# Moving rows of a zero store from behind a GpSimd copy to in front of it

## The chip, the cores and the metric

The kernel runs on one core of a Trainium2 chip. The metric is the device time of one execution in microseconds (us): the median of several runs, beside the profile of one more execution. Engines are named as in the profile: PE (TensorE), DVE (VectorE), ACT (ScalarE), POOL (GpSimd), SP (SyncE, which here does nothing but issue transfers). Data move in DMA transfers; a transfer is split into packets, which run on the core's 16 DMA engines. A transfer signals its end on a semaphore.

## The reference: what is computed

A decoding step of an attention block over a sliding window of cached keys and values, beside a gated feed-forward block, and the gradients of the sum of both with respect to eight inputs. Cut to what matters:

```python
x = A_x                                   # (4, 1, 512)
xn = _layernorm(x, axis=-1)
out = x + _A_ref(xn, A_k_cache, A_v_cache, A_wq, A_wo) \
        + _B_ref(xn, B_w_gate, B_w_up, B_w_down)
# _A_ref: only the last W = 1024 of 4096 cached keys take part
k = jnp.repeat(k_cache[:, :, Sk - W:, :], rep, axis=1)
v = jnp.repeat(v_cache[:, :, Sk - W:, :], rep, axis=1)
...
_out, _vjp = jax.vjp(_f, ...)             # outputs: out and the gradients
```

Two of the nine outputs are the gradients of the two caches, `out_2` (keys) and `out_3` (values), each of 4 batches x 8 heads x 4096 keys x 128 numbers of 2 bytes. The first 3072 keys of each head lie outside the window, so their gradient is zero and must be written as zeros: 50 MB of the 81 MB that the kernel writes.

## The kernel before, in words

First comes the feed-forward block (forward and gradients), then the attention in four passes of the loop over `t`, each with two heads of the cache: `kv_steps` (scores), `softmax`, `kv_steps` again, `softmax_d`, `odq`, and `dvdk` and `dw`, whose pieces are put on a list (`bg`) and called between other work by `tick`. All loads and stores go out in the order of the program text, since the schedule is written by hand (`manual_schedule`). SP issues nearly all of them, from its own queue (q1 in the profile); GpSimd issues the later weight loads and the stores of this change on another (q0).

The zeros come from one tile in on-chip memory, `ztile`, 128 partitions x 6144 numbers of zeros. `zlist` holds 32 entries, each two heads of `out_2` or `out_3`: 1536 KB. `zero(n)` takes the next n and has SP store them; calls of it are strewn over the whole kernel. Thirty of the 32 go out so. `zero_15` (L166 to L187), called once in the last pass (L763), takes the last two entries out of the list, four heads of `out_3` of the last batch, called h = 0 to 3 here. It works with units of 192 keys (`KR`): the first `k0` = 2880 keys are 15 such rows, one unit is left of each head.

- Of h = 0, 1 and 2 the first 2880 keys are copied by GpSimd from the heads of `out_2[0]` that were zeroed long before: 15 rows x 3 heads x 49,152 bytes, from memory to memory (the 15-row copy).
- The unit of 192 keys left of each of these heads is stored from `ztile`, partly by GpSimd, in rows of 16 keys (4096 bytes), partly by SP at the end of the program, 16 rows of some keys each.
- h = 3 is stored whole by SP at the end, in 128 rows of 24 keys.

`rest(eng, n, h, k0, w)` is one such store: `n` rows of `w` keys of head `h`, from key `k0`. With fewer than 128 rows it reads every eighth partition of `ztile`. In the kernel before, GpSimd issues a store of 5 rows (80 keys of h = 0), the copy, and a store of 12 rows (the 192 keys of h = 1). `zero_15` returns a list of functions, called behind the last pass (L781, after `tick(len(bg))` and `zero(len(zlist))`), in which SP stores h = 3, the other 112 keys of h = 0, and the 192 keys of h = 2. `store` (L100 to L107) is the helper through which each goes, so in the profile all of them stand at L103. The stores of the results proper (`stg_dv`, `stg_dk`, `osb_o`, `osb_q`) come from the pieces, also at L103.

Of the kernel before, what the change touches and what calls it, by code (L numbers as in the profile page):

```python
# [14 lines left out]
P = 128  # L15
# [3 lines left out]
def kernel(  # L19
# [28 lines left out]
    nc = tc.nc  # L48

    B, Sq, D = A_x.shape  # L50
    _, G, Sk, Dh = A_k_cache.shape
# [4 lines left out]
    K0 = Sk - W  # L56
# [43 lines left out]
    def store(eng, out, in_, kind):  # L100

        eng.nop()
        d = eng.dma_start(out=out, in_=in_)  # L103
        for k in ("rest", "zeros") if kind == "rest" else ("rest",):
            tc.declare_no_dep(d.ins, group=k, reason="stores write disjoint parts of the outputs")
        tc.add_to_no_dep_group(kind, d.ins)
        return d  # L107
# [50 lines left out]
    ztile = const.tile([P, ZW], BF16, name="ztile")  # L158
# [7 lines left out]
    def zero_15():  # L166


        last = [z for z in zlist if z[0] is out_3][-2:]
        for z in last:  # L170
            zlist.remove(z)
        b, g = last[0][1:]
        assert last[1][1:] == (b, g + ZR)
        dst = out_3[b, g:g + 2 * ZR]
        KR = K0 // 16
        k0 = 15 * KR

        def rest(eng, n, h, k0, w):
            store(eng, dst[h, k0:k0 + n * w, :].rearrange("(m j) d -> m (j d)", m=n), ztile[0:n if n == P else 8 * n - 7:1 if n == P else 8, 0:w * Dh],
                  "zeros")  # L180

        rest(nc.gpsimd, 5, 0, k0, 16)
        s_, d_ = (x[0:3, 0:k0, :].rearrange("g (m j) d -> m g (j d)", m=15) for x in (out_2[0], dst))
        store(nc.gpsimd, d_, s_, "zeros")
        rest(nc.gpsimd, 12, 1, k0, 16)
        return [lambda: rest(nc.sync, P, 3, 0, K0 // P), lambda: rest(nc.sync, 16, 0, k0 + 80, 7),
                lambda: rest(nc.sync, 16, 2, k0, 12)]  # L187


    nc.gpsimd.memset(ztile[:], 0.0)  # L190
# [512 lines left out]
    for f4 in range(NF4):  # L703
        held = {}
        n = min(4, NF - 4 * f4)
# [34 lines left out]
    with tc.tile_pool(name="kv_b", bufs=GP, reuse_waits="tile") as kv_b, \  # L740
# [7 lines left out]
        for t in range(NT):  # L748
# [13 lines left out]
            if t == NT - 1:  # L762
                rest = zero_15()  # L763
# [81 lines left out]
```

## Time and profile before

| what | value |
|---|---|
| median of three runs | 284.18 us (284.09 to 284.64) |
| the profiled execution | 284.17 us |
| its span (first to last instruction) | 282.4 us |
| PE, DVE, ACT, POOL busy | 72%, 58%, 42%, 15% of the span |
| DMA | 112.12 MB, mean 397 GB/s; busy share 0.9 or more in 36 of 40 slices |
| SP's queue (q1) and GpSimd's (q0) | 101.28 and 8.57 MB |
| GpSimd's issues: 5 rows, copy, 12 rows | at 224.43, 224.98 and 225.61 us |
| last compute instruction (`dx_b`, DVE) | ends at 260.8 us |
| SP's last four issues | 266.09, 266.69, 268.01 and 269.26 us |
| end of SP's waiting for the last landings | 281.2 us |

How to read it: the span runs from the first to the last instruction of one execution, times are counted from its start. A line such as "out_dram<-ztile POOLq DMA_DIRECT2D x1, 48.0 KB, 16.9" is one kind of transfer: what it writes and reads, the engine whose queue issued it, how many, the size, and the us from its issue to its landing. `out_dram<-out_dram` is the copy. The packet records of the trace list each packet's queue, start, duration and bytes, but not which of the 16 DMA engines moved it; this can be followed from the order of sizes, since an engine takes up its next packet when the one before ends.

### The profile page before, as it was taken

The numbers are of one execution on the slowest core, as the hardware profiler recorded it, in microseconds if no ns is written. First come the engines' busy times: TensorE is split into PE (matmuls) and PEld (weight loads), VectorE is DVE, ScalarE is ACT, GpSimd is POOL, SyncE is SP. The second block draws the span as 40 slices with busy tenths as digits, with TensorE's granted clock in tenths as the row PEclk, the third lists the DMA queues.
The fourth block names the chain that finished last, engine by engine and source line by source line (L and its number), as shares of the span: only waits on it lengthen the run. The fifth ranks groups of instructions, "written<-read, shape, count | busy, mean of one in ns | idle before, by whom it ended". The sixth has DMA issues, their size and how long they took to land.

```text
span 282.4 us, 6862 instructions
## 1 busy us (share of the span) xinstructions
PE 202.5 (72%) x2962; PEld 138.7 (49%) x2972; DVE 164.4 (58%) x313; ACT 117.7 (42%) x219; POOL 41.9 (15%) x43
## 2 busy tenths in 40 slices
PE   0274799949789889998999199898999599272000
PEld 0263576735456675556765066676555574031000
DVE  7947546645776655577666158767677638178000
ACT  2031486635035418753547155353866048161000
POOL 8600000007002250002340000232000600000000
PEclk9999589986999999999999869999999979958555
DMA  7999999999999999999999999999899998999990
GB/s 265 395 375 430 430 426 419 425 424 414 379 393 429 412 425 421 422 421 421 415 422 414 418 425 423 422 370 399 367 371 414 393 396 357 424 430 427 410 417 38
DMA packets 19613, 112.12 MB, mean 397 GB/s; under 512 B 1746, under 2 KB 4594, under 8 KB 11347
## 3 DMA queue, kind: packets, MB, share of 16 engines
q1 hardware_dynamic: 17664, 101.28, 87.2%
q0 software_dynamic: 1760, 8.57, 7.7%
q10 hardware_dynamic: 160, 1.84, 1.8%
q8 instruction: 23, 0.38, 0.5%
q14 instruction: 6, 0.05, 0.0%
HBM read 32.89 MB, written 81.01 MB: 403 GB/s over the span
## 4 chain that ended last, share of the span: by engine, by line
PE 43%; DMA 26%; DVE 16%; ACT 4%; issue 2%; SPq 0%; DVEq 0%; ACTq 0%
DMA out_dram<-stg_dv 13%; PE T_ps L302 8%; PE kv_ps L507 6%; DMA wd_sb<-in_B_w_down_dram 6%; PE S_ps L368 5%; PE od_ps L473 5%; DMA out_dram<-osb_g 4%; DMA out_dram<-osb_d 3%; DVE T_sb L98 3%; PE dwq_ps L543 2%; DVE dS_s L390 2%; PE acc_ps L279 2%; DVE P_s L390 2%; PE dwo_ps L528 2%; PE pT_ps L302 2%
## 5 line engine op out<-in xcount | busy, mean ns | idle before, releaser
L98 DVE COPY T_sb<-T_ps 128x1024 bf16<-128x1024 bf16 x64 | 44.1, 689 | 26.9 <-PE T_ps L302 26.7
L97 ACT CAST stg_dk<-kv_ps 128x512 bf16<-128x512 f32 x52 | 29.0, 589 | 33.5 <-DMA out_dram<-stg_dv 14.3
L97 ACT CAST stg_dv<-kv_ps 128x512 bf16<-128x512 f32 x51 | 28.1, 588 | 25.1 <-PE kv_ps L507 24.6
L507 PE MATMUL kv_ps<-qmr,dS_s 128*128 128x512 bf16 x62 | 23.3, 412 | 13.3 <-ACT stg_dk L97 12.6
L486 POOL TENSOR_TENSOR o_s<-od_r,msk_r 128x512 bf16<-128x512 bf16 x8 | 9.1, 1158 | 110.4 <-DVE od_r L478 81.1
L302 PE MATMUL T_ps<-ident,vb 128*128 128x128 bf16 x256 | 20.5, 226 | 0.6 <-DVE T_sb L98 0.4
L302 PE MATMUL T_ps<-ident,kb 128*128 128x128 bf16 x256 | 20.6, 226 | 0.2 <-issue 0.2
L302 PEld LDWEIGHTS <-kb 128*128 128x128 bf16 x256 | 17.6, 102 | 4.5 <-issue 1.5
L302 PEld LDWEIGHTS <-vb 128*128 128x128 bf16 x256 | 17.4, 102 | 5.0 <-issue 3.2
L507 PE MATMUL kv_ps<-domr,P_s 128*128 128x512 bf16 x58 | 19.7, 382 | 0.1
L97 ACT CAST osb_q<-dwq_ps 128x512 bf16<-128x512 f32 x25 | 14.6, 586 | 8.6 <-PE dwq_ps L543 7.6
L352 POOL TENSOR_TENSOR domr<-r,msk 128x1024 bf16<-128x1024 bf16 x4 | 7.6, 1892 | 71.2 <-DVE r L349 65.1
L97 ACT CAST osb_g<-dwg_ps 128x512 bf16<-128x512 f32 (+1 forms) x25 | 12.3, 545 | 12.5 <-PE dwg_ps L696 5.7
L98 DVE CAST stg_dk<-kv_ps 128x512 bf16<-128x512 f32 x12 | 8.1, 689 | 14.0 <-DMA out_dram<-stg_dv 13.4
L97 ACT CAST osb_o<-dwo_ps 128x512 bf16<-128x512 f32 x24 | 13.9, 586 | 4.6 <-PE dwo_ps L528 3.8
L98 DVE COPY wgT<-wgT_ps 128x1024 bf16<-128x1024 bf16 x14 | 9.6, 687 | 7.3 <-PE wgT_ps L302 7.3
L507 PEld LDWEIGHTS <-dS_s 128*128 128x128 bf16 x64 | 6.2, 101 | 14.5 <-issue 13.4
L368 PE MATMUL S_ps<-T_sb,qm 128*32 128x256 bf16 x128 | 12.7, 387 | 0.6 <-DVE T_sb L98 0.5
L368 PE MATMUL S_ps<-T_sb,dom 128*32 128x256 bf16 x128 | 12.7, 387 | 0.1
L528 PE MATMUL dwo_ps<-dyr,o_s 128*128 128x512 bf16 x32 | 12.6, 420 | 0.3 <-ACT stg_dk L97 0.2
L98 DVE COPY woT<-woT_ps 128x1024 bf16<-128x1024 bf16 x16 | 11.0, 687 | 2.9 <-PE woT_ps L302 2.5
L543 PE MATMUL dwq_ps<-od_r,xnm 128*128 128x256 bf16 x64 | 11.9, 285 | 0.2 <-ACT osb_q L97 0.2
(190 smaller groups left out, 384.6 us busy)
## 6 DMA issues: line engine op xcount, KB each, us to landing
out_dram<-ztile SPq DMA_DIRECT2D x30, 1536.0 KB, 19.4
kb<-in_A_k_cache_dram SPq DMA_DIRECT2D x8, 1024.0 KB, 20.2
vb<-in_A_v_cache_dram SPq DMA_DIRECT2D x8, 1024.0 KB, 21.7
out_dram<-stg_dv SPq DMA_DIRECT2D x8, 1024.0 KB, 16.6
out_dram<-stg_dk SPq DMA_DIRECT2D x8, 1024.0 KB, 19.4
out_dram<-osb_o SPq DMA_DIRECT2D x8, 512.0 KB, 16.1
out_dram<-osb_q SPq DMA_DIRECT2D x8, 512.0 KB, 19.3
out_dram<-osb_g SPq DMA_DIRECT2D x8, 448.0 KB, 11.8
```

The costliest lines, as they stand in the source:

```text
L97: return nc.scalar.copy(out=out, in_=in_)
L98: return nc.vector.tensor_copy(out=out, in_=in_)
L279: nc.tensor.matmul(ps[:, c, :], lhsT=lf(c), rhs=rhs, start=(k == 0), stop=(k == len(terms) - 1))
L302: nc.tensor.transpose(ps[:, i, :], a, ident[:])
L352: nc.gpsimd.tensor_tensor(out=mr[:].rearrange("p g q d -> p (g q) d"), in0=r4[:, k, :].unsqueeze(1).broadcast_to([P, SL, Dh]), in1=msk[:]. ...
L368: nc.tensor.matmul(ps[b * RB:(b + 1) * RB, :], lhsT=zt[:, b * GP + g, c0:c0 + RB], rhs=T_sb[:].rearrange("p (x b) -> p b x", b=B)[:, b, :] ...
L390: nc.vector.scalar_tensor_tensor(out=out[:], in0=src[:].unsqueeze(2).broadcast_to([P, WQ, B]), scalar=rr[:, 0:1], in1=mskb[:].unsqueeze(1) ...
L473: nc.tensor.matmul(od_ps[g * 32:g * 32 + B * rep, k, g, :], lhsT=cols[:, jj, g * NQ + q, :], rhs=blks[(t, g)][:, j, :], start=(j == 0), st ...
L486: nc.gpsimd.tensor_tensor(out=o_s[:, g], in0=rows[:, g].unsqueeze(1).broadcast_to([P, rep, Dh]), in1=msk_r[:].unsqueeze(2).broadcast_to([P ...
L507: nc.tensor.matmul(mps[:].rearrange("p q d -> p (q d)"), lhsT=src[:, j * P:(j + 1) * P], rhs=mr[:, g].rearrange("p q d -> p (q d)"), start ...
L528: nc.tensor.matmul(mps[:], lhsT=o_s[:, g].rearrange("p r d -> p (r d)")[:, i:rep * Dh:rep], rhs=dyr[:], start=True, stop=True)
L543: nc.tensor.matmul(mps[:, i].rearrange("p g d -> p (g d)"), lhsT=xnm[:, i2 * 2 + i, c * P:(c + 1) * P], rhs=dq_r[:].rearrange("p g d -> p ...
```

## The change

GpSimd issues stores of 9 rows (144 keys of h = 0) and 8 rows (128 keys of h = 1) and then the copy; nothing behind it. What is left of the three units goes out on SP at the end: 16 rows of 3 keys (48 keys of h = 0), of 4 keys (64 keys of h = 1) and of 12 keys (192 keys of h = 2), behind the 128 rows of h = 3. GpSimd's rows of 4096 bytes are 17 in both kernels, and SP's bytes are the same; SP has one transfer more. SP's stores of 16 rows read partitions 0 to 15 of `ztile` instead of every eighth; GpSimd's still read every eighth. The other engines' instructions and their order are the same.

```diff
         k0 = 15 * KR
+        used = [0, 0, 0]
 
         def rest(eng, n, h, k0, w):
-            store(eng, dst[h, k0:k0 + n * w, :].rearrange("(m j) d -> m (j d)", m=n), ztile[0:n if n == P else 8 * n - 7:1 if n == P else 8, 0:w * Dh],
-                  "zeros")
-
-        rest(nc.gpsimd, 5, 0, k0, 16)
+            src = ztile[0:8 * n - 7:8] if n < 16 else ztile[0:n]
+            store(eng, dst[h, k0:k0 + n * w, :].rearrange("(m j) d -> m (j d)", m=n), src[:, 0:w * Dh], "zeros")
+
+        for h, n in enumerate((9, 8)):
+            rest(nc.gpsimd, n, h, k0, 16)
+            used[h] = n * 16
         s_, d_ = (x[0:3, 0:k0, :].rearrange("g (m j) d -> m g (j d)", m=15) for x in (out_2[0], dst))
         store(nc.gpsimd, d_, s_, "zeros")
-        rest(nc.gpsimd, 12, 1, k0, 16)
-        return [lambda: rest(nc.sync, P, 3, 0, K0 // P), lambda: rest(nc.sync, 16, 0, k0 + 80, 7),
-                lambda: rest(nc.sync, 16, 2, k0, 12)]
+        return [lambda: rest(nc.sync, P, 3, 0, K0 // P)] + [
+            lambda h=h: rest(nc.sync, 16, h, k0 + used[h], (KR - used[h]) // 16) for h in range(3)]
```

## The prediction, made before the result was known

> **What bounds the kernel now.** I read the page from its end backwards, since the change touches only the last zero stores. First the stretches of the last 20 us (columns: stretch, its length, busy us and count of each engine, the granted clock PEclk, the mean busy share of the 16 DMA engines, GB/s):
>
> ```profile
> 262.00:273.00 11.00, 0.00 (x0) 0.00 (x0) 0.00 (x0) 0.00 (x0) 0.00 (x0) 0.50 1.02 420
> 273.00:276.00 3.00, 0.00 (x0) 0.00 (x0) 0.00 (x0) 0.00 (x0) 0.00 (x0) 0.50 0.84 347
> 276.00:277.20 1.20, 0.00 (x0) 0.00 (x0) 0.00 (x0) 0.00 (x0) 0.00 (x0) 0.50 0.14 58
> 277.20:280.40 3.20, 0.00 (x0) 0.00 (x0) 0.00 (x0) 0.00 (x0) 0.00 (x0) 0.50 0.06 25
> 280.40:282.40 2.00, 0.00 (x0) 0.00 (x0) 0.00 (x0) 0.00 (x0) 0.00 (x0) 0.50 0.00 0
> ```
>
> From 262 us no compute engine has work; the DMA engines drain stores. From 277.2 the share is 0.06, which is one engine in sixteen: **for 3.2 us a single DMA engine is still writing, and the kernel ends when it does.** The transfers of that stretch say what it writes:
>
> ```profile
> DMA packets 15, 0.08 MB, mean 25 GB/s; under 512 B 3, under 2 KB 4, under 8 KB 13
> ...
> q1 hardware_dynamic: 15, 0.08, 5.9%
> ```
>
> q1 is SP's queue: the share this engine has of SP's last four stores. Every one of those is cut evenly over the sixteen engines, so this engine has no more to do, it is late. I followed the packet records (start, duration, bytes) backwards, each engine's SP packets being the same row of sizes in the same order. Fifteen engines end at 273.35 to 277.19 us, fourteen of them between 275.3 and 277.2; the last ends at 280.44. From 242 us on it has no gap at all, and it was late before: of the 512 KB store issued at 219.54, the median engine lands at 222.21 and the last at 227.35, 5.1 behind. So the end moves by what is added to or taken from **this one engine's packets**, called the late engine below. Anything else has slack.
>
> Now the transfers of GpSimd's queue, 224.3 to 225.7 (operation, count, KB, us from issue to landing):
>
> ```profile
> out_dram<-out_dram POOLq DMA_DIRECT2D x1, 2160.0 KB, 16.7
> out_dram<-ztile POOLq DMA_DIRECT2D x1, 48.0 KB, 16.9
> out_dram<-ztile POOLq DMA_DIRECT2D x1, 20.0 KB, 8.2
> ```
>
> These are the copy of 15 rows, the 12-row store and the 5-row store. The copy puts three packets of 49,152 B on each of 15 engines and none on one; that one finishes first of all, at 273.35. On the late engine the three took 1.94 + 2.36 + 1.89 = 6.19 us; the commonest duration is 1.815, so 5.45 is the floor. **So the copy is the largest thing that GpSimd's queue puts on the late engine, and the question of this change is whether it still does.**
>
> **Which engine is left out.** Rows in front of the copy could turn the assignment of rows to engines, and 5 rows become 9 + 8 = 17. The records answer for the kernel before. The five packets of the 5-row store fall on five engines that all carry the copy, the late engine among them (4096 B at 229.26, 0.17 us, then a copy packet at 230.56). The twelve packets of the 12-row store all follow a third copy packet on their engine; three engines carry the copy but no packet of the 12, and the fourth without one is the engine left out. If each transfer began where the one before ended, the 12-row store would begin on the very engine that the copy left out. It does not. All three fit one picture: row 0 always goes to the same engine, row 1 to the next; 5 rows are engines 1 to 5 of that order, 12 rows 1 to 12, 15 rows 1 to 15, and the 16th is left out. The small stores of ScalarE (4 rows) lie on four of the five engines of the 5-row store, so the late engine is the fifth.
>
> The Trainium skill, page "DMA: Bandwidth & Descriptors", section "Why a DMA increments its semaphore by 16 and not by 1", states that transfers issued by GpSimd on fewer than 16 engines take consecutive engines from a round-robin cursor, and, as an exception measured for some direct copies, all 16 with the rows dealt from engine 0 up. The trace agrees with the exception (12 packets, none on the engine that the copy left out). By the main rule the fifth engine was left out before and the first would be after, the fifth then gaining the copy's three packets: an estimate from that page's rule and the 6.19 us of the trace is 284.2 + 6.2 = 290.4. It speaks against the change, but the late engine carries the copy already, so I do not sum by it.
>
> **The change part by part.** The profiled execution took 284.17 us, span 282.4 and 1.8 around it; the median of the three runs is 284.18, so sums on the profile carry over unchanged.
>
> 1. *GpSimd's issues.* Gone: one of 0.56 us before the copy, one of 0.55 behind it. New: two of 0.55 before it. The copy is issued 0.55 later (224.98 to 225.5) and its first packet comes about 0.5 later than 230.56. Behind it on GpSimd's queue nothing is left but the end of the program, and only the end waits for its landing, 241.68 now, 39 us before the late engine is through. Cost 0; without that cover 0.55.
> 2. *GpSimd's rows.* 5 + 12 = 17 of 4096 B become 9 + 8 = 17. The fifth engine has one packet of each store, two before and two after: 0. Were the late engine sixth to eighth, it would be +0.16 (one packet at 0.159), tenth to twelfth -0.16. I take 0 and keep both.
> 3. *SP's stores.* 128 rows, 16 x 7 keys, 16 x 12 keys become 128 rows, 16 x 3, 16 x 4, 16 x 12: the same bytes, one issue more. SP's last issues take 1.21 to 1.33 us, and the last ends at 269.26 + 1.33 = 270.6. One more makes 271.9; if it also waits for an earlier store's completion by reusing its semaphore (the store of 254.08 lands at 271.40), 272.7. The late engine reaches its packet of the last store at 280.31: 7.6 us of cover. The other engines reach theirs at 273.3 to 277.1. Cost 0; without cover 1.3 to 2.1.
> 4. *SP's packets on the late engine.* One of 1792 B (0.074 us) becomes 768 B and 1024 B, and one completion of 0.009 is added. From 0.074 and 0.121 (3072 B) a byte costs 0.037 ns, so the two take 0.036 + 0.046: +0.02 together. SP's stores of 16 rows also read partitions 0 to 15 now, not every eighth one; a packet that runs alone, as these do on the late engine, has no neighbour to collide with: 0, and at most the 0.12 that the longest of them takes.
> 5. *Completions at the end.* The late engine's last packets of the three final stores end 0.08 and 0.12 apart, but their landings stand at 280.64, 280.83 and 281.02, **0.19 apart each**. One store more adds between 0.02 and 0.19; I take 0.19, the row that shows this very thing, and it contains the 0.02 of item 4. SP's end waits once for each semaphore, 0.06 a step; two such steps stand behind 281.02 now. If the added store uses one of them, it is no longer behind: -0.06.
> 6. *Contention.* The copy's packets meet SP's stores 0.5 us later, on the same engines. On the late engine they can be as short as the floor, 5.45 - 6.19 = -0.74, or as stretched as the worst first packet on any engine (3.26 against 1.94): +1.32. Nothing in the trace says which way half a microsecond turns it. I take 0.
>
> Sum: 0 + 0 + 0 + 0.19 - 0.06 = **+0.13: 284.3 us**, bounds of items 2 and 6 aside. A measurement here can tell about 0.2%, 0.57 us, from no change: 283.6 to 284.75 counts as the same.
>
> **The rivals.**
> *Faster: the rows in front move the engine left out onto the late one.* For it: something picks the engine, and 17 rows end one place past where 16 would, 5 rows four places past. Against it: the packets above line up from one engine whatever went before. Price: the late engine loses 6.19, to 274.25; the engine left out until now gains at least 5.45, from 273.35 to 278.8 (with 6.19, 279.5). The end moves from 280.44 to 278.8 to 279.5, so -0.9 to -1.6, and with +0.13 the time is 282.7 to 283.4, near 283.0. If the place moves anywhere else, the late engine keeps its 280.44 and nothing changes. A milder way to the same side is item 6 at its floor: -0.74 + 0.13 = 283.6.
> *Slower: the copy's packets are stretched on the late engine.* Place: 230.5 to 236 us, where all engines alternate copy packets with SP's stores; just ahead of it, at 228.9, SP's packets of 12,288 B took up to 1.0 us instead of 0.46. For it: two engines of fifteen had first packets of 3.14 and 3.26, and the late engine has no gap in which to make it up. Against it: the late engine's own already ran 0.74 over the floor. Price +1.32 + 0.13: 285.6; from 0.44 more than today's 6.19 on it leaves the band of no change.
> *No engine moves, though rows were put in front:* that is the forecast.
>
> **How the numbers follow.** Forecast, 284.3 and within 0.2%: 0.54. Slower, by stretched packets up to 285.6: 0.28. Faster, 0.18: 0.10 for the moved engine (283.0), 0.08 for the floor (283.6). The forecast's own range is 283.7 to 284.75. To leave out no more than 2 in 10 the range goes down to the middle of the moved engine's times and up nearly to the stretched end: 283.0 to 285.4.
>
> **What would show it.** Right: one DMA engine alone at the end for about 3 us (share 0.06), ending near 280.5, SP's last issue near 272, four landings 0.19 apart, and the first engine to finish still near 273.4. The moved engine: the lone stretch shrinks to 1.6 to 2.5 us and ends by 279.5. Stretched: the lone stretch grows past 4 us, with copy packets over 6.6 us on that engine. Wrong altogether: several engines still busy after 277.5, or a gap in the late engine's packets while it waits for SP's last issues.

## The result, and the profile after

The changed kernel took 284.65 us (median of four runs, 284.18 to 285.18) and the kernel before, beside it, 284.38 (four runs, 284.09 to 284.64): ratio 1.001, interval 0.9989 to 1.0032. That is no change that a measurement here can tell, and 0.35 above the forecast of 284.3. The profiled execution of the changed kernel took 284.70, its span 283.0; the one before 284.17 and 282.4.

The stretches of the end, changed kernel, columns as in the prediction:

```profile
262.00:273.00 11.00, 0.00 (x0) 0.00 (x0) 0.00 (x0) 0.00 (x0) 0.00 (x0) 0.50 1.01 419
273.00:276.00 3.00, 0.00 (x0) 0.00 (x0) 0.00 (x0) 0.00 (x0) 0.00 (x0) 0.50 0.74 301
276.00:277.20 1.20, 0.00 (x0) 0.00 (x0) 0.00 (x0) 0.00 (x0) 0.00 (x0) 0.50 0.15 59
277.20:280.40 3.20, 0.00 (x0) 0.00 (x0) 0.00 (x0) 0.00 (x0) 0.00 (x0) 0.50 0.06 25
280.40:283.00 2.60, 0.00 (x0) 0.00 (x0) 0.00 (x0) 0.00 (x0) 0.00 (x0) 0.50 0.01 4
```

The fourth line is the same as before: for these 3.2 us one engine in sixteen writes. What it writes, from the transfers of that stretch:

```profile
DMA packets 11, 0.08 MB, mean 25 GB/s; under 512 B 1, under 2 KB 1, under 8 KB 8
...
q1 hardware_dynamic: 11, 0.08, 5.9%
```

Again SP's queue alone. It is eleven packets instead of fifteen, because the engine is a little less far at 277.2. Followed back from the end, the late engine ends at 280.86 (280.44 before), the next at 277.16, and the first to finish at 273.16.

GpSimd's transfers issued from 224 to 226 us, changed kernel:

```profile
out_dram<-out_dram POOLq DMA_DIRECT2D x1, 2160.0 KB, 16.7
out_dram<-ztile POOLq DMA_DIRECT2D x1, 36.0 KB, 8.5
out_dram<-ztile POOLq DMA_DIRECT2D x1, 32.0 KB, 9.0
```

The stores of 9 and 8 rows are there, and the copy takes the same 16.7 us. It is still left out on one engine, the one that finishes first. The late engine still carries the copy, in packets of 1.94 + 2.62 + 1.88 = 6.44 us (6.19 before).

SP's last issues (start, duration of the group, engine, line, operation), changed kernel:

```profile
262.41 1.73 SPq L103 DMA_DIRECT2D out_dram<-osb_q  x2
265.90 6.25 SPq L103 DMA_DIRECT2D out_dram<-ztile  x5
```

Five issues where there were four, the last of them from 271.84 to 272.15. It waited for a landing at 271.82, that of the store issued at 254.52, whose semaphore it reuses. The late engine came to its packet of this fifth store only at 280.73, so the wait cost nothing. The four last landings stand at 281.10, 281.28, 281.47 and 281.66.

GpSimd's last issues, changed kernel:

```profile
224.16 1.17 POOL L103 DMA_DIRECT2D out_dram<-ztile  x2
225.32 0.60 POOL L103 DMA_DIRECT2D out_dram<-out_dram  x1
```

The copy is issued at 225.32. Its first packet on any engine starts at 230.81, 0.25 later than before; on the late engine the first starts at 231.38, 0.83 later. Behind it GpSimd issues nothing.

### The profile page after: what moved, and what is told of

It reads as the page before. It is cut to its first block, busy times and chain, and to the rows that moved or that the text cites. A ratio compares the mean times of both kernels' runs of the same rounds, so it can differ in the third digit from the quotient of the medians.

```text
span 283.0 us, 6873 instructions
## 1 busy us (share of the span) xinstructions
PE 203.6 (72%) x2972; PEld 139.2 (49%) x2972; DVE 163.8 (58%) x313; ACT 117.6 (42%) x219; POOL 41.9 (15%) x43
## 4 chain that ended last, share of the span: by engine, by line
DMA 52%; PE 24%; DVE 8%; ACT 4%; issue 1%; POOL 1%; SPq 0%; DVEq 0%; ACTq 0%
DMA out_dram<-stg_dv 21%; DMA out_dram<-osb_o 12%; DMA wq_sb<-in_A_wq_dram 7%; DMA wd_sb<-in_B_w_down_dram 6%; DMA out_dram<-osb_g 4%; PE kv_ps L509 4%; PE od_ps L475 3%; DMA out_dram<-osb_d 3%; PE T_ps L304 3%; PE S_ps L370 2%; PE wdT_ps L304 2%; PE dwq_ps L545 1%; PE acc_ps L281 1%; DVE dS_s L392 1%; ACT osb_d L97 1%
## 5 line engine op out<-in xcount | busy, mean ns | idle before, releaser
L509 PE MATMUL kv_ps<-domr,P_s 128*128 128x512 bf16 x64 | 21.1, 378 | 0.0
L304 PE MATMUL T_ps<-ident,kb 128*128 128x128 bf16 x256 | 20.0, 222 | 0.0
```

What stands on the lines that cost most here:

```text
L304: nc.tensor.transpose(ps[:, i, :], a, ident[:])
L509: nc.tensor.matmul(mps[:].rearrange("p q d -> p (q d)"), lhsT=src[:, j * P:(j + 1) * P], rhs=mr[:, g].rearrange("p q d -> p (q d)"), start ...
```

## The experiments

Two things are asked. First, is it really one engine's packets that set the end, and are the terms of the sum (an added landing, the order, the extra issue) of the sizes given? Second, why did 17 rows in front of the copy not change which engine the copy leaves out? The first theory is the prediction's: row 0 of every transfer with fewer rows than engines goes to the same engine, always. Its rival is a running place: each transfer starts on the engine behind the last one of the transfer before it. Each number below is the median of the runs named, with the ratio to the kernel before on the same chip.

### One late engine, and the parts of the change

**Bytes taken from the late engine, four rows added on others.** An extra GpSimd copy of 1536 keys of h = 3 goes behind the 15-row copy, in 4 rows, which by the first theory miss the fifth engine; SP's store of h = 3 shrinks from 24 to 12 keys in each row.

```diff
+        KX, NX = K0 // 2, 4
+        s_, d_ = (x[h, 0:KX, :].rearrange("(a m j) d -> m a (j d)", m=NX, j=KR) for x, h in ((out_2[0], 0), (dst, 3)))
+        store(nc.gpsimd, d_, s_, "zeros")
-        return [lambda: rest(nc.sync, P, 3, 0, K0 // P), ...
+        return [lambda: rest(nc.sync, P, 3, KX, (K0 - KX) // P), ...
```

> The kernel before, but half of h = 3 (1536 keys) is written by GpSimd, as a second copy of 4 rows x 2 x 192 keys right behind the 15-row copy; SP's last big store shrinks to the other half (128 rows of 12 keys). Theory (rows always start on the same engine, the fifth is late and sets the end): the late engine loses 4 packets of 6144 B, 4 x 0.234 = 0.92 us; the first four engines gain two packets of 49,152 B less 0.92, 2.7 us, and have about 4.7 of slack: 284.4 - 0.9 = 283.5, with the lone engine at the end for less than 3 us. Rival 1 (a round-robin cursor): behind 5 and 15 rows the next transfer starts on the fifth engine, so the late one gets two packets more: +2.7, 287.1. Rival 2 (the sum of all bytes sets the end): no change, 284.4.

Measured: 283.86 us (11 runs), ratio 0.9982, interval 0.9973 to 0.999. In its profile the late engine ends at 279.78, and the lone stretch is lone no more; the same stretch as above:

```profile
277.20:280.40 3.20, 0.00 (x0) 0.00 (x0) 0.00 (x0) 0.00 (x0) 0.00 (x0) 0.50 0.15 60
```

Share 0.15 instead of 0.06: three engines with extra rows, now ending at 278.87 to 279.05, have joined it. Taking bytes from the late engine moves the end. But only three of the four expected engines had gained anything, a first sign against the first theory; the fourth ended at 275.3.

**The same keys in eight rows, thus on the late engine too.** As above with `NX = 8`.

> The same 1536 keys in 8 rows x 192 keys instead of 4 x 2 x 192. Theory: the rows fall on the first eight engines, one packet of 49,152 B each, the late fifth among them: +1.82 - 0.92 = +0.9, 285.3, 1.8 us more than with 4 rows. If the late engine were not among the first eight: 283.5. Sum of bytes: 284.4, as with 4 rows.

Measured: 285.32 us (5 runs), ratio 1.0035, interval 1.0022 to 1.0049. It missed its purpose. Eight rows of one unit each are one contiguous block, and it went out as sixteen packets of 24,576 bytes, one on every engine, so no engine was chosen. The one profile, of its fastest run (284.25), shows the late engine ending at 280.41, as before. What the other 0.85 us is, it does not show.

**The order alone.** The 12-row store goes in front of the copy; nothing else changes.

```diff
         rest(nc.gpsimd, 5, 0, k0, 16)
+        rest(nc.gpsimd, 12, 1, k0, 16)
...
-        rest(nc.gpsimd, 12, 1, k0, 16)
```

> The order alone: GpSimd issues the store of 12 rows in front of the copy too, behind the one of 5; SP's stores stay as they were. Theory: no engine's share changes, 284.4, within 0.3; the copy's first packet about 0.5 us later; the same engine is left out and finishes first near 273.3. Rival (17 rows in front turn the engine left out): the engine that finishes first gets the copy and another loses it; 282.7 to 283.4 if that is the late one, 284.4 otherwise, and then the first to finish ends near 270.

Measured: 284.44 us (11 runs), ratio 0.9998, interval 0.9987 to 1.0008. The late engine ends at 280.49, the first to finish at 273.51: no place moves.

**The added store at the end alone.** SP's 16 rows of 7 keys become 16 of 3 and 16 of 4.

```diff
-        ..., lambda: rest(nc.sync, 16, 0, k0 + 80, 7),
+        ..., lambda: rest(nc.sync, 16, 0, k0 + 80, 3), lambda: rest(nc.sync, 16, 0, k0 + 128, 4),
```

> SP's part alone: the 112 keys of h = 0 go out as two stores of 16 rows, 3 and 4 keys each (every eighth partition as before); GpSimd as before. Theory: +0.19 for one more landing and -0.06 for one step less behind it: +0.13, 284.5; the last SP issue near 272, waiting for the store of 254 us to land. Rival (SP's issue is on the path): +1.3 or more, 285.7.

Measured: 284.56 us (11 runs), ratio 1.0004, interval 0.9995 to 1.0013: +0.09, where the sum has +0.13; the measurement cannot tell it from nothing. In the profile the late engine ends at 280.40 and the landings stand at 280.63, 280.81, 281.00 and 281.19, so the 0.19 a landing is seen again.

**The changed kernel again.**

> The changed kernel again, for a narrower interval. Theory: +0.13, between 284.4 and 284.8. Rival (the order in front of the copy is worth nothing and the added SP store is hidden too): 284.4 within 0.1.

Measured: 285.04 us (12 runs), ratio 1.0012, interval 0.9998 to 1.0027: +0.41. Its profile has the late engine at 280.70, the first to finish at 273.49, the landings 0.19 apart and SP's last issue at 271.67.

### Which engine a copy begins on

**Five rows, on the late engine by the first theory.** The extra copy takes 1920 keys of h = 3 as 5 rows x 2 x 192.

```diff
+        KX, NX = 1920, 5
+        s_, d_ = (x[h, 0:KX, :].rearrange("(a m j) d -> m a (j d)", a=2, m=NX) for x, h in ((out_2[0], 0), (dst, 3)))
+        store(nc.gpsimd, d_, s_, "zeros")
-        return [lambda: rest(nc.sync, P, 3, 0, K0 // P), ...
+        return [lambda: rest(nc.sync, P, 3, KX, (K0 - KX) // P), ...
```

> The kernel before, but 1920 keys of h = 3 are written by GpSimd right behind the 15-row copy, as 5 rows x 2 x 192 keys; SP's last big store shrinks to 128 rows of 9 keys. (The 8 rows of the run before lay end to end in memory and went out as 16 packets of 24,576 B, one on every engine, so that run did not ask what it was meant to.) Theory (rows always start on the same engine, the late one is the fifth): it gains two packets of 49,152 B, 2 x 1.815, and loses 1920 x 256 / 16 = 30,720 B of SP's, 5 packets of 0.23: 3.63 - 1.15 = +2.5, 286.9. If the late engine is not among the first five: -1.15 at most, about 283.3. Round-robin cursor (start on the fifth engine): it is hit as well, +2.5.

Measured: 283.44 us (12 runs), ratio 0.9966, interval 0.9951 to 0.9981. Faster, where the first theory had the late engine loaded further. The copies of this kernel (KB, us to landing):

```profile
out_dram<-out_dram POOLq DMA_DIRECT2D x1, 2160.0 KB, 16.4
...
out_dram<-out_dram POOLq DMA_DIRECT2D x1, 480.0 KB, 18.2
```

Both are on GpSimd's queue, as meant, and the second was cut into ten packets of 49,152 bytes. The stretches of the end:

```profile
276.00:277.20 1.20, 0.00 (x0) 0.00 (x0) 0.00 (x0) 0.00 (x0) 0.00 (x0) 0.50 0.29 118
277.20:278.40 1.20, 0.00 (x0) 0.00 (x0) 0.00 (x0) 0.00 (x0) 0.00 (x0) 0.50 0.13 52
278.40:280.40 2.00, 0.00 (x0) 0.00 (x0) 0.00 (x0) 0.00 (x0) 0.00 (x0) 0.50 0.03 12
```

The late engine is through at 279.49, having only lost bytes. The four with extra packets that are busy behind 277.2 (they end at 277.50 to 277.76) are the four that carry ScalarE's small stores, engines 1 to 4 of the prediction's order. The two packets of the fifth row lie early, on the engine that the 15-row copy had left out. So the second copy began on the sixteenth engine, right behind the fifteenth. **For copies the first theory falls.**

**Four rows with packets of a size of their own.** 1920 keys as 4 rows x 2 x 240, packets of 61,440 bytes, which the records tell apart from all others. The edit is the one above with `NX = 4`.

> The same 1920 keys as 4 rows x 2 x 240 keys (packets of 61,440 B). Theory: the fifth engine only loses, -1.15, less the 0.3 by which the first run with 4 rows fell short: 283.3 to 283.6; the first four engines gain 2 x 2.27 - 1.15 = 3.4 and end near 279, a little ahead of it. 3.3 us less than with 5 rows. Round-robin cursor: the start on the fifth engine hits it, 4.54 - 1.15 = +3.4, 287.8. Sum of bytes: as with 5 rows.

Measured: 283.49 us (12 runs), ratio 0.9959, interval 0.9945 to 0.9974. Two of the eight packets start early, at 234.66 and 237.90, on the engine left out; six, starting from 238.84 to 241.77, lie on three of the four ScalarE-store engines, which end at 279.10 to 279.31. The late engine still ends last, at 279.38. Sixteenth, first, second, third: the running place again, and it explains the three engines of the first experiment too.

**Copies in front and behind, 5 + 15 + 12 rows.** All zeros of h = 0 to 2 are copied. With a running place for copies, 5 copied rows in front make the 15-row copy begin on the sixth engine and leave out the fifth, the late one.

```diff
+        def rows(n, k, w):
+            s_, d_ = (x[0:3, k:k + n * w, :].rearrange("g (m j) d -> m g (j d)", m=n) for x in (out_2[0], dst))
+            store(nc.gpsimd, d_, s_, "zeros")
+        for n, k, w in ((5, k0, 24), (15, 0, KR), (12, k0 + 120, 6)):
+            rows(n, k, w)
+        return [lambda: rest(nc.sync, P, 3, 0, K0 // P)]
```

> All GpSimd transfers of zeros copy from memory to memory: 5 rows x 3 heads x 24 keys in front, the 15-row copy, 12 rows x 3 heads x 6 keys behind; SP stores only h = 3. New theory, formed on the run with 5 rows: a copy from memory starts on the engine behind the last one of the copy before it, while a store from the tile always starts on the first engine and does not move that place; the late engine is the fifth. So 5 copied rows in front make the 15-row copy start on the sixth engine and leave out the fifth, the late one. It loses 6.19 us and gains 3 packets of 6144 B and 3 of 1536 B, 0.9, less 0.9 for two rows, two SP stores and their landings: it ends near 274.3. The sixteenth, free of the copy until now, ends at 273.35 - 1.33 of gaps + 6.2 = 278.2, and the next latest at 277.2 + 0.9: the end moves from 280.4 to about 278, 282.0. Old theory (every transfer starts on the first engine): the sixteenth is left out still, the late engine ends where it did, 284.3.

Measured: 281.09 us (5 runs), ratio 0.9868, interval 0.9846 to 0.989. The stretches of the end, of its slowest run (281.74):

```profile
276.00:277.20 1.20, 0.00 (x0) 0.00 (x0) 0.00 (x0) 0.00 (x0) 0.00 (x0) 0.50 0.24 97
277.20:278.40 1.20, 0.00 (x0) 0.00 (x0) 0.00 (x0) 0.00 (x0) 0.00 (x0) 0.50 0.05 20
278.40:280.40 2.00, 0.00 (x0) 0.00 (x0) 0.00 (x0) 0.00 (x0) 0.00 (x0) 0.50 0.00 0
```

Nothing is written behind 278.4. The last engine ends at 278.21, the next at 277.17.

**The same with 17 copied rows in front, 9 + 8 + 15.** The changed kernel's numbers of rows, but as copies. The place comes to the second engine, so the first is left out, which helps nobody.

```diff
-        for n, k, w in ((5, k0, 24), (15, 0, KR), (12, k0 + 120, 6)):
+        for n, k, w in ((9, k0, 16), (8, k0 + 144, 6), (15, 0, KR)):
```

> The same, but 9 rows x 3 heads x 16 keys and 8 rows x 3 heads x 6 keys in front and nothing behind: the rows of the changed kernel, as copies from memory. New theory: 17 rows move the start to the second engine, so the first is left out and finishes first; it was never late. The late engine carries the copy, gains 0.7 in small packets and loses 0.9 with two rows, two SP stores and their landings: 284.3, no gain, 2.3 more than with 5 rows. Old theory: 284.3 as well, but the engine that finishes first is not one of the four that carry ScalarE's small stores. If the number of SP stores alone made the run with 5 rows faster, this one is as fast.

Measured: 284.17 us (12 runs), ratio 0.9983, interval 0.9968 to 0.9998. The stretches of the end:

```profile
276.00:277.20 1.20, 0.00 (x0) 0.00 (x0) 0.00 (x0) 0.00 (x0) 0.00 (x0) 0.50 0.21 87
277.20:278.40 1.20, 0.00 (x0) 0.00 (x0) 0.00 (x0) 0.00 (x0) 0.00 (x0) 0.50 0.05 20
278.40:280.40 2.00, 0.00 (x0) 0.00 (x0) 0.00 (x0) 0.00 (x0) 0.00 (x0) 0.50 0.07 28
```

The lone engine is back: the last line is 0.07 where the 5-row kernel had 0.00. It ends at 280.83, and the first to finish (273.46) is now one of the ScalarE-store engines. The two kernels copy the same bytes and differ in how the rows are cut; 3.1 us lie between their medians. The remaining -0.6 (interval -0.9 to -0.1) was not tested by itself. Two final landings fewer than in the kernel before would give about -0.4 of it (2 x 0.19).

**Only what moves the place.** 5 copied rows in front, the 15-row copy, nothing behind; the other 112 keys of each head are stored by SP in 16 rows of 7.

```diff
-        for n, k, w in ((5, k0, 24), (15, 0, KR), (12, k0 + 120, 6)):
+        for n, k, w in ((5, k0, 16), (15, 0, KR)):
             rows(n, k, w)
-        return [lambda: rest(nc.sync, P, 3, 0, K0 // P)]
+        return [lambda: rest(nc.sync, P, 3, 0, K0 // P)] + [
+            lambda h=h: rest(nc.sync, 16, h, k0 + 80, 7) for h in range(3)]
```

> The run with 5 copied rows in front, without the 12 copied rows behind: 5 rows x 3 heads x 16 keys and the 15-row copy on GpSimd, the 112 keys left of each of h = 0, 1 and 2 as three SP stores of 16 rows x 7 keys. The copied rows of one execution are 20, not 32. If the place at which a copy starts is set anew for each execution: the late engine is left out every time, it ends near 274.5, the last one near 278.3, and three landings instead of one stand at the end, +0.4: 281.5 to 282.4, the 12 rows behind were not needed. If the place is carried from one execution to the next, it moves by 4 each time, the late engine is left out in one of four, and the median is that of the kernel before, 284.3 to 284.8, with single runs near 282.

Measured: 280.76 us (6 runs, 279.69 to 281.84), ratio 0.9849, interval 0.9816 to 0.9883: 4.1 us under the kernel before and the best version here. Its copies, the stretches of its end, and SP's last issues:

```profile
out_dram<-out_dram POOLq DMA_DIRECT2D x1, 2160.0 KB, 17.0
...
out_dram<-out_dram POOLq DMA_DIRECT2D x1, 60.0 KB, 9.1
```

```profile
273.00:276.00 3.00, 0.00 (x0) 0.00 (x0) 0.00 (x0) 0.00 (x0) 0.00 (x0) 0.50 0.86 355
276.00:277.20 1.20, 0.00 (x0) 0.00 (x0) 0.00 (x0) 0.00 (x0) 0.00 (x0) 0.50 0.06 24
277.20:280.40 3.20, 0.00 (x0) 0.00 (x0) 0.00 (x0) 0.00 (x0) 0.00 (x0) 0.50 0.01 3
```

```profile
262.33 5.89 SPq L103 DMA_DIRECT2D out_dram<-ztile  x5
```

No store writes in what was the lone stretch (the 0.01 is one packet of another queue); all sixteen engines end between 275.16 and 276.72. SP's last issues begin at 262.33 instead of 266.09, since what SP waits for comes sooner. The store of `stg_dv` issued near 234 us stands in both kernels in the chain that leads to the last compute (start, duration; the kernel before first, then this one):

```profile
233.86 13.93 DMA out_dram<-stg_dv
```

```profile
234.01 10.40 DMA out_dram<-stg_dv
```

It lands at 247.8 in the kernel before and at 244.4 here. In the kernel before fifteen engines had landed their share by 244.91, and the last one at 247.79; here the fifteenth and the last landed at 243.83 and 244.41.

### Less GpSimd work

**All zeros on SP** (`rest = zero_15()` becomes `zero()`; the two entries stay in the list).

> GpSimd stores no zeros at all; the two entries of the list go out on SP like the other thirty, one where the copy stood, the other at the end. Theory: the late engine loses the copy (6.19) and two packets of 4096 B (0.33), and gains its sixteenth of 2228 KB, 142,592 B or 11.6 packets of 0.46 = 5.3 us: -1.2, 283.2; -0.4 if the copy cost it only its floor of 5.45. The engine that was left out gains 5.3, from 273.35 to 278.7, and stays ahead. The lone engine at the end stays, then, with less than 3 us to itself. Rival (the engine left out is what the copy is good for, and the end follows the mean load): the mean stays, 284.4; or, if stores of results land later behind the longer SP queue, slower than 285.

Measured: 283.21 us (6 runs), ratio 0.9953, interval 0.9937 to 0.9969. The late engine still ends last, at 279.68, the others at 274.48 to 275.78.

**SP's zeros with a 4-row copy alone.** No 15-row copy; 4 rows x 2 x 240 keys of the last head are copied (`zero_4` issues that) and SP stores all else.

```diff
-                rest = zero_15()
+                rest = zero_4()
+                zero()
```

> No 15-row copy: the zeros go out on SP, but for 1920 keys that GpSimd copies in 4 rows x 2 x 240 keys. Theory: the late engine loses 1.2 as in the run with all zeros on SP and 1.15 as in the run with 4 rows of 240 keys; the first four engines gain 3.4 and end near 278.7, above the late one's 278.1: -1.8, 282.7. If both savings are the same one: 283.2.

Measured: 282.29 us (6 runs), ratio 0.992, interval 0.9895 to 0.9945. The late engine ends at 278.24, the four that carry the copy at 277.45 to 277.77, the rest at 272.3 to 273.4. In both kernels the late engine ends earlier and is still the last: 0.76 and 2.2 sooner, with 1.4 and 2.5 off the time. Both also have fewer small stores at the end, which was not separated.

## Why the prediction was right, and where its reason was not

**What bounds the kernel: right.** In every profile above but those of the two kernels that leave it out of the copy, this engine ends last. The order alone and the added store alone moved neither its end (280.49, 280.40) nor the time. The five other kernels that took bytes from it and gave them to other engines gained 0.6 to 2.5 us.

**Items 1 to 3: right.** GpSimd's later copy (first packet +0.25 on the earliest engine and +0.83 on the late one, against the +0.5 given), its 17 rows and SP's fifth issue cost nothing that shows. The wait by reuse came as written, at 271.84, and stayed 8 us under cover.

**Items 4 and 5: right in kind.** On the late engine the packets of 768, 1024 and 3072 bytes took 0.036, 0.046 and 0.121 us, read from partitions 0 to 15 here and from every eighth with the added store alone: the sizes of item 4, and no price for the partitions. Four landings stand 0.18 to 0.19 apart, alone and in the change, and one step of 0.06 is gone from the end. The part alone measured +0.09 (interval -0.14 to +0.37).

**Item 6: not settled.** The changed kernel measured +0.27 and +0.41 against the +0.13 of the sum, and both intervals contain the sum. The copy's packets on the late engine took 6.44 and 6.37 in the two profiles of the changed kernel and 6.35 with the order alone, against 6.24 with the added store alone and 6.19 before. So where the copy is issued later its packets were 0.16 to 0.25 longer, a term that the sum had at nothing; it lies well inside the bounds of item 6, and single profiles do not settle it. The engine's place before that also differs from one execution to the next. At the store issued at 219.26 it was 5.49 behind the median, against 5.14 before, ahead of anything the change touches, and in the other profiles 4.8 to 6.3. There it was itself only 0.12 later than before (227.47 against 227.35). That and the copy's 0.25 are 0.37 of the 0.42 by which its end moved in the profile. The slower rival asked for copy packets over 6.6 us and a lone stretch past 4; neither came.

**"Which engine is left out": the number held, the rule failed.** The step read "row 0 always goes to the same engine, row 1 to the next; 5 rows are engines 1 to 5 of that order, 12 rows 1 to 12, 15 rows 1 to 15, and the 16th is left out". For stores from the tile in on-chip memory that stands: the kernel with 17 of them in front leaves out the same engine as the one with 5. For copies from memory to memory it is false: each begins on the engine behind the last one of the copy before it, and stores from the tile in front of it do not move that place. With a single multi-row copy both rules leave out the sixteenth engine, so the kernel before could not tell them apart. The packets that I argued from were those of the 12-row store, and the claim about the copy was carried over from them. That the forecast still held was luck in this: the change puts only stores from the tile in front, for which the rule stands. For copied rows in front it would have named the wrong engine.

The Trainium skill, page "DMA: Bandwidth & Descriptors", section "Why a DMA increments its semaphore by 16 and not by 1", has both: a running place among the engines, and some direct copies dealt from engine 0. I accepted the exception and set the main rule aside for all of GpSimd's transfers. The runs give the exception to the stores from the tile and the main rule to the copies (281.09 with 5 copied rows in front, 284.17 with 17). The 290.4 estimated from the main rule for this change came from moving the place by rows of the tile, which move nothing.

**The faster rival: real, but not by this change, and its price too small.** The place can be moved onto the late engine, by copies. Its term was the engine left out until now, set to end at 278.8 to 279.5 once it has the copy, for 282.7 to 283.4. With the 5 copied rows the time was 281.09 and 280.76, a gain of 3.7 and 4.1 where this rival had 0.9 to 1.6. Its sum held all else still, and all else did not stay still: in the second of them the landing of the `stg_dv` store came 3.4 us sooner, SP's last stores went out 3.8 us earlier, and the engine newly loaded ended no later than 276.72. That last is seen in the profiles; how much of the extra each of the two gives was not separated.

**Open.** Every copy here that went out by rows has two or three blocks in each row, and every store of a few rows from the tile has one, so whether the source or the number of blocks decides which rule a transfer follows was not separated. Why the late engine is 5 us behind by 219 us was not tried, nor what the eight-row kernel's +0.85 is. That the four-row kernel gained 0.6 instead of more also has no cause shown.

## What to carry to other kernels

When the end is one DMA engine's backlog, count packets by engine before counting bytes: here the same copied bytes, cut into 5 or 17 rows in front, were 3.1 us apart. A transfer with fewer rows than engines loads some engines more, and where it began depended here on its kind, so read the place from packets of that very kind, from a kernel in which two of them follow each other. And a change that frees a late engine frees the waits on its landings too, so price it with those.

## What was not expected of the hardware

- As far as these runs show, the place from which copies go on is set anew in each execution. The last version moves it by 20 rows, four past a whole turn; kept from one execution to the next, it would leave out the late engine in one of four, but all six runs took 279.69 to 281.84.
- A copy whose rows are contiguous is cut again: eight rows of 49,152 bytes went out as sixteen packets of 24,576, one on each engine.
- Small completions one behind the other on one engine land 0.18 to 0.21 us apart, though their packets end 0.04 to 0.12 apart.
- Storing all zeros from the tile (283.21) was 1.4 us faster than having GpSimd copy 15 rows (284.63 beside it).
